# Linear attention and a two-layer MLP on one core: block 0 split after twelve weight groups, and a second buffer for the key exponentials

## The chip, the core and the metric

One core of a Trainium2 chip runs the whole program. The metric is the device time in microseconds (us) of one execution. Engines are named as the profile names them: PE is TensorE (matmuls), PEld its weight loads, DVE is VectorE, ACT is ScalarE, POOL is GpSimd, SP is SyncE (here it only starts DMAs).

## What is computed

Linear attention over 8 batches, 8 heads, 576 tokens and a head width of 64, and then a two-layer MLP on the 4608 tokens of width 512, with a hidden width of 2048 and a leaky ReLU between the layers.

```python
def phi(x):
    proj = np.einsum('bhsd,df->bhsf', x, w_phi)                  # 128 features
    proj = proj - np.max(np.abs(proj), axis=-1, keepdims=True)
    return np.concatenate([np.exp(proj), np.exp(-proj)], axis=-1)
q_p, k_p = phi(q), phi(k)
kv = np.einsum('bhsf,bhsd->bhfd', k_p, v)
z = np.sum(k_p, axis=2)
num = np.einsum('bhsf,bhfd->bhsd', q_p, kv)
den = np.einsum('bhsf,bhf->bhs', q_p, z)[..., None] + 1e-06
x = (num / den), heads side by side, as (4608, 512)
h = x @ w_in
out = np.maximum(0.01 * h, h) @ w_out
```

## The kernel before

**Attention** goes by pairs of heads: 32 pairs, four to a batch. Pairs 0 to 3 have functions of their own at the start. From pair 4 on `k_phase(i)` makes the key side of pair i while `q_phase(i - 1)` (`token_q_phase` below pair 8) makes the query side of the pair before it. A key phase works through 576 tokens in five chunks `c` of 128 (the last of 64). For each it subtracts the maximum (into `pmk`), takes exp of plus and minus that on ACT into the tile `ek` (L249, L250), rounds `ek` to `kph` on ACT (L69, called with the key "kph"), takes the rest `kpl` = `ek` - `kph` on POOL or DVE (L74), and multiplies both by the values on PE (L211). From pair 8 on this is done in such high and low parts; before that `ek`, `kph` and `kpl` serve as three exponential buffers. `ek` has one buffer and is also used for the sums that leave PSUM (`kvs`). The tile `kvx` (same size) holds the key-value product of pairs 5 and 7 and is not used after pair 7.

A query phase ends with its products on PE (L417, L418, L420), copies to `ring` and `tq` on ACT (L422, L423), two transposes and a reciprocal on DVE (L426, L428, L429) and a multiplication into `ring` on POOL (L74). `ring` holds the attention output of two batches (576 tokens by 512 each).

**The MLP** goes by blocks of 256 tokens (18 blocks) and by groups `ft` of 128 hidden units (16 groups). A step is one block and one group. `layer1` is 12 matmuls of 256 columns (L601, L602, L604: high by high, high by low, low by high), then leaky ReLU and rounding on ACT (L607, L69 "gh") and the rest on DVE (L609 "gl"). `layer2`, three steps later (`LAG`), is six matmuls of 512 columns into `acc` (L623, L624, L625). Before a block starts, `split` rounds its 256 tokens out of `ring` into `xh` (ACT) and `xl` (POOL). A block can start only when the attention of every batch it touches is finished: block 2 needs batch 1 (pairs 4 to 7), block 4 needs batch 2 (pairs 8 to 11), block 6 batch 3.

**The weights** arrive as float64, in 32 pieces, alternately of `w_in` (`w0`) and `w_out` (`w1`), two for each group `ft`. `load_weights` decodes each on ACT and DVE and writes a high part (`w0h`, `w1h`, L69 on ACT) and a low part (`w0l`, `w1l`, L74 on DVE). The number in `w0h2` is `ft` divided by 4.

**The order of the work**: the table `steps` sets the order of the MLP steps. It runs `CUT` groups of block 0, then all 16 of block 1, then the rest of block 0, then blocks 2 to 17. The partial sum of block 0 is held in the `ks` buffer (`held`) in between, and block 0 is split a second time. A scheduler then puts all instructions into one fixed sequence for each engine; attention has the higher priority, then the weights, and the MLP steps fill in. Each engine runs its sequence in order.

```python
CUT = 8
steps = [(0, ft) for ft in range(CUT)] + [(1, ft) for ft in range(NFT)] + [(0, ft) for ft in range(CUT, NFT)] + steps
```

Of the kernel before, what the change touches and what calls it, by code (L numbers as in the profile page):

```python
# [9 lines left out]
F32 = mybir.dt.float32  # L10
# [7 lines left out]
P = 128  # L18
# [9 lines left out]
NTOK = B * S  # L28
NBLK = NTOK // T
LAG = 3  # L30
CUT = 8
NN = 8
NK = 8
NF = 12
# [12 lines left out]
def attention_moe_kernel(ctx: ExitStack, tc: tile.TileContext, q, k, v, vt, w_phi, w_in, w_out, out):  # L47
# [8 lines left out]
    def st(shape, dt, tag):  # L56
        return sp.tile(shape, dt, tag=tag, name=tag, bufs=BUFS.get(tag, 1))
# [8 lines left out]
    def copy_(key, o, i):  # L66
        e = pick(key) or "a"
        if e == "a":
            nc.scalar.copy(o, i)  # L69
        else:  # L70
            (nc.vector if e == "v" else nc.gpsimd).tensor_copy(o, i)

    def tt_(key, o, a, b, op):
        (nc.vector if pick(key) == "v" else nc.gpsimd).tensor_tensor(o, a, b, op=op)  # L74
# [68 lines left out]
    for j in range(2):  # L143
        r = slice(64 * j, 64 * j + 64)
        c = slice(F * j, F * j + F)
# [45 lines left out]
    def k_phase(i):  # L191
        nat, plain = i < NK, i < NF
# [17 lines left out]
        def kv_mm(j, lt, rt, first=False, last=False):  # L210
            nc.tensor.matmul(kvp[0 : lt.shape[1], 256 * j : 256 * j + 256], lhsT=lt, rhs=rt,  # L211
                             start=first and j == 0, stop=last, skip_group_check=True)

        for g in range(3):
# [30 lines left out]
            yield  # L245
            for s in range(w):
                c = 2 * g + s
                ek = st([P, 2, 256], F32, ("ek", "kph", "kpl")[c % 3] if nat else "ek")
                nc.scalar.activation(ek[r, :, 0:F], pmk[r, 2 * s : 2 * s + 2], AF.Exp)  # L249
                nc.scalar.activation(ek[r, :, F:256], pmk[r, 2 * s : 2 * s + 2], AF.Exp, scale=-1.0)  # L250
                if nat:
                    for j in range(2):
                        kv_mm(j, rv[r, 4 * j + c if c < 4 else 8 + j], ek[r, j], first=c == 0, last=c == 4)
                    yield
                    continue
                if c < 4:
                    kph = st([P, 2, 256], F32R, "kph")
                    kpl = st([P, 2, 256], F32R, "kpl")
                    copy_("kph", kph, ek)
                    tt_("kpl", kpl, ek, kph.bitcast(F32), ALU.subtract)  # L260
                    for j in range(2):
                        kv_mm(j, vh[:, 4 * j + c], kph[:, j], first=c == 0)
                        kv_mm(j, vl[:, 4 * j + c], kph[:, j])
                    for j in range(2):
                        kv_mm(j, vh[:, 4 * j + c], kpl[:, j])
                else:
                    kst = st([P, 2, 256], F32R, "kph")
                    copy_("kst", kst[r], ek[r])
                    nc.vector.tensor_tensor(kst[0:64], ek[r], kst[r].bitcast(F32), op=ALU.subtract)
                    for j in range(2):  # L270
                        kv_mm(j, vl[:, 8 + j], kst[:, j])
                        kv_mm(j, vh[:, 8 + j], kst[:, j], last=True)
                yield
# [340 lines left out]
    def layer2(i, ft, half=range(TT)):  # L614
        first, last = (ft in (0, CUT), ft in (CUT - 1, NFT - 1)) if i == 0 else (ft == 0, ft == NFT - 1)
        if first and half[0] == 0:
# [11 lines left out]
        for t in half:  # L628
            if ft == CUT - 1:
                if t == 0:  # L630
# [39 lines left out]
    steps = [(i, ft) for i in range(2, NBLK) for ft in range(NFT)]  # L670
    steps = [(0, ft) for ft in range(CUT)] + [(1, ft) for ft in range(NFT)] + [(0, ft) for ft in range(CUT, NFT)] + steps
    split(0)
# [47 lines left out]
```

## Time and profile before

| what | value |
|---|---|
| median of 3 runs (lowest, highest) | 1194.11 us (1193.7, 1196.47) |
| the profiled execution: its own time, its span | 1196.45 us, 1194.7 us |
| PE busy | 1164.5 us, 97% |
| PEld busy | 1045.5 us, 88% |
| ACT busy | 833.5 us, 70% |
| DVE busy | 755.9 us, 63% |
| POOL busy | 417.5 us, 35% |
| mean granted TensorE clock | 0.994 of 2.4 GHz |

A busy PE in this profile is not PE at its peak: the records of matmuls overlap, since one starts before the one ahead of it has ended. How fast PE goes is read from the distance between two starts, or from the number of matmul records in a stretch of known length. A matmul with plain float32 operands stands as two records. A figure in square brackets behind a row is the time in which the engine was idle just before it, with the instruction whose end released it.

### The profile page before, as it was taken

What the parts mean: (1) busy time and instruction counts of PE and PEld (TensorE: products, weight loads), DVE (VectorE), ACT (ScalarE), POOL (GpSimd) and SP (SyncE); (2) the same over time, 40 slices, a digit from 0 to 9 for tenths busy, and PEclk for the clock granted to TensorE, in tenths of its full rate; (3) what the DMA queues carried; (4) which work ended last, traced back from release to release, by engine and by line L of the source; (5) the groups of instructions that cost most, each with busy time, mean ns of one, the idle gap of its engine ahead of it and who ended that gap; (6) DMA issues with size and microseconds to landing.
All of it is one profiled execution on the core that took longest, in us unless ns stands there. A gap on an engine that the chain in (4) does not pass through costs nothing.

```text
span 1194.7 us, 21190 instructions
## 1 busy us (share of the span) xinstructions
PE 1164.5 (97%) x7576; PEld 1045.5 (88%) x7576; DVE 755.9 (63%) x1510; ACT 833.5 (70%) x2108; POOL 417.5 (35%) x422
## 2 busy tenths in 40 slices
PE   8899999999998999999999999999999999999998
PEld 5687888899897989889899999998999999988987
DVE  4899883566767777677787777726777776111111
ACT  4898884667777787878788888837787877432232
POOL 0111011345454444545455454604454544110000
PEclk9899999999998999999999999999999999999999
DMA  7334532111201111110111111101011100000000
GB/s 208 90 101 142 152 114 59 40 42 31 60 22 50 32 50 31 41 30 22 50 31 50 32 49 32 49 12 37 23 50 32 49 1 19 1 18 19 1 19 18
DMA packets 62778, 57.01 MB, mean 48 GB/s; under 512 B 45136, under 2 KB 46288, under 8 KB 62672
## 3 DMA queue, kind: packets, MB, share of 16 engines
q1 hardware_dynamic: 62672, 55.65, 16.4%
q8 instruction: 60, 0.98, 0.4%
q14 instruction: 46, 0.38, 0.1%
HBM read 46.20 MB, written 9.44 MB: 47 GB/s over the span
## 4 chain that ended last, share of the span: by engine, by line
PE 82%; DVE 8%; ACT 5%; issue 2%; DMA 1%; POOL 1%; SPq 0%; DVEq 0%; ACTq 0%; POOLq 0%
PE h L601 10%; PE h L604 10%; PE h L602 10%; PE acc L623 10%; PE acc L625 10%; PE acc L624 10%; PE c L211 7%; PE a L302 2%; PE a L420 2%; PE a L418 2%; PE a L417 2%; PE a L231 2%; PE a L333 1%; PE a L377 1%; PE a L378 1%
## 5 line engine op out<-in xcount | busy, mean ns | idle before, releaser
L601 PE MATMUL h<-xh,w0h 128*128 128x256 f32 x1152 | 296.3, 287 | 5.9 <-DVE gl L609 4.9
L602 PE MATMUL h<-xh,w0l 128*128 128x256 f32 x1152 | 290.9, 282 | 0.0
L609 DVE TENSOR_TENSOR gl<-h,gh 128x256 fp32r<-128x256 f32 x288 | 118.7, 416 | 245.9 <-ACT gh L69 220.6
L623 PE MATMUL acc<-w1h,gh 128*128 128x512 f32 x576 | 229.6, 399 | 6.4 <-ACT gh L69 6.3
L601 PEld LDWEIGHTS h<-xh,w0h 128*128 128x128 f32 x1152 | 218.0, 189 | 17.0 <-DVE gl L609 8.0
L624 PE MATMUL acc<-w1l,gh 128*128 128x512 f32 x576 | 227.7, 395 | 0.0
L602 PEld LDWEIGHTS h<-xh,w0l 128*128 128x128 f32 x1152 | 217.9, 189 | 7.0 <-issue 0.4
L607 ACT ACTIVATE h<-h 128x256 f32<-128x256 f32 x288 | 105.3, 368 | 155.0 <-PE h L604 152.0
L625 PE MATMUL acc<-w1h,gl 128*128 128x512 f32 x576 | 204.4, 396 | 0.0
L604 PE MATMUL h<-xl,w0h 128*128 128x256 f32 x1152 | 200.3, 283 | 0.0
L74 POOL TENSOR_TENSOR ql<-eq,qh 128x576 fp32r<-128x576 f32 x96 | 146.5, 1539 | 73.6 <-ACT qh L69 51.0
L604 PEld LDWEIGHTS h<-xl,w0h 128*128 128x128 f32 x1152 | 164.5, 189 | 1.1 <-issue 0.4
L74 POOL TENSOR_TENSOR kpl<-ek,kph 128x512 fp32r<-128x512 f32 x72 | 96.6, 1342 | 146.9 <-PE c L211 67.2
L623 PEld LDWEIGHTS acc<-w1h,gh 128*128 128x128 f32 x576 | 108.4, 188 | 27.7 <-ACT gh L69 8.9
L624 PEld LDWEIGHTS acc<-w1l,gh 128*128 128x128 f32 x576 | 108.4, 188 | 18.0
L69 ACT CAST gh<-h 128x256 fp32r<-128x256 f32 x288 | 105.1, 371 | 25.6 <-PE acc L624 20.0
L74 POOL TENSOR_TENSOR xl<-ring,xh 128x256 fp32r<-128x256 f32 (+3 forms) x100 | 62.6, 655 | 162.1 <-PE h L604 131.6
L74 POOL TENSOR_TENSOR ring<-ring,mb 128x576 f32<-128x576 f32 (+2 forms) x45 | 49.8, 1108 | 192.9 <-DVE mb L559 39.2
L625 PEld LDWEIGHTS acc<-w1h,gl 128*128 128x128 f32 x576 | 99.3, 189 | 8.1
L249 ACT ACTIVATE ek<-pmk 128x256 f32<-128x256 f32 (+1 forms) x128 | 53.3, 417 | 33.5 <-POOL kpl L74 17.3
L199 DVE TENSOR_TENSOR ks<-rk,ks 64x576 fp32r<-64x576 f32 x40 | 44.5, 1112 | 30.5 <-ACT ks L69 29.9
L211 PE MATMUL c<-kph,vh 128*66 128x256 f32 x240 | 62.1, 281 | 0.7 <-ACT kph L69 0.7
(214 smaller groups left out, 2257.8 us busy)
## 6 DMA issues: line engine op xcount, KB each, us to landing
out_dram<-o SPq DMA_DIRECT2D x35, 256.0 KB, 2.1
rk<-in_k_dram SPq DMA_DIRECT2D x29, 288.0 KB, 2.8
ring<-in_w_in_dram SPq DMA_DIRECT2D x16, 512.0 KB, 3.6
qh<-in_w_out_dram SPq DMA_DIRECT2D x16, 512.0 KB, 3.7
rq<-in_q_dram SPq DMA_DIRECT2D x28, 288.0 KB, 3.0
rv<-in_v_dram SPq DMA_DIRECT2D x29, 256.0 KB, 3.5
rv<-in_vt_dram SPq DMA_DIRECT2D x58, 32.0 KB, 3.0
fr<-in_k_dram SPq DMA_DIRECT2D x2, 288.0 KB, 3.4
```

The costliest lines, as they stand in the source:

```text
L69: nc.scalar.copy(o, i)
L74: (nc.vector if pick(key) == "v" else nc.gpsimd).tensor_tensor(o, a, b, op=op)
L211: nc.tensor.matmul(kvp[0 : lt.shape[1], 256 * j : 256 * j + 256], lhsT=lt, rhs=rt, start=first and j == 0, stop=last, skip_group_check=True)
L249: nc.scalar.activation(ek[r, :, 0:F], pmk[r, 2 * s : 2 * s + 2], AF.Exp)
L601: nc.tensor.matmul(ph, lhsT=weight(0, "h", ft)[:, d * P : d * P + P], rhs=xh[:, d], start=d == 0, stop=False)
L602: nc.tensor.matmul(ph, lhsT=weight(0, "l", ft)[:, d * P : d * P + P], rhs=xh[:, d], start=False, stop=False)
L604: nc.tensor.matmul(ph, lhsT=weight(0, "h", ft)[:, d * P : d * P + P], rhs=xl[:, d], start=False, stop=d == NP - 1)
L607: nc.scalar.activation(ph, ph, AF.Prelu, alpha=0.01)
L609: nc.vector.tensor_tensor(gl, ph, gh.bitcast(F32), op=ALU.subtract)
L623: nc.tensor.matmul(a, lhsT=gh[:, ts], rhs=weight(1, "h", ft), start=first, stop=False)
L624: nc.tensor.matmul(a, lhsT=gh[:, ts], rhs=weight(1, "l", ft), start=False, stop=False)
L625: nc.tensor.matmul(a, lhsT=gl[:, ts], rhs=weight(1, "h", ft), start=False, stop=last)
```

## The change

There are two edits. `CUT` goes from 8 to 12, so that twelve groups of block 0 run ahead of block 1 and four after it. And for key phases of pairs above 8 (`NN` is 8) the exponentials of odd chunks go to the tile `kvx` in place of `ek`; even chunks keep `ek`.

```diff
-CUT = 8
+CUT = 12
...
-                ek = st([P, 2, 256], F32, ("ek", "kph", "kpl")[c % 3] if nat else "ek")
+                ek = st([P, 2, 256], F32, ("ek", "kph", "kpl")[c % 3] if nat else "kvx" if c % 2 and i > NN else "ek")
```

The number of instructions is the same on every engine; the scheduler puts them in another order. Up to the eighth step of the MLP the order of PE is unchanged. Three places follow.

First place: PE, behind the end of the eighth step's `layer1` (rows with buffer numbers; `gh_1676` is the eighth step's result, `w0h0` is the high part of groups 0 to 3, `w0h2` that of groups 8 to 11). Before:

```order
L302 MATMUL a_1136<-bd_73,rq_604 128x256 x2
L211 MATMUL c_1071<-ek_1089,rv_1002 66x256 x2
L211 MATMUL c_1071<-kph_1103,rv_1002 66x256 x2
L601 MATMUL h_1695<-xh_70,w0h0_616 128x256
L602 MATMUL h_1695<-xh_70,w0l0_617 128x256
L601 MATMUL h_1695<-xh_70,w0h0_616 128x256
```

Now:

```order
L211 MATMUL c_1071<-kph_1103,rv_1002 66x256 x2
L623 MATMUL acc_1583<-w1h1_721,gh_1676 128x512
L624 MATMUL acc_1583<-w1l1_722,gh_1676 128x512
L623 MATMUL acc_1584<-w1h1_721,gh_1676 128x512
L624 MATMUL acc_1584<-w1l1_722,gh_1676 128x512
L625 MATMUL acc_1583<-w1h1_721,gl_1677 128x512
L625 MATMUL acc_1584<-w1h1_721,gl_1677 128x512
L601 MATMUL h_1687<-xh_70,w0h2_800 128x256
L602 MATMUL h_1687<-xh_70,w0l2_801 128x256
```

The ninth step was group 0 of block 1 and is now group 8 of block 0, behind six matmuls of `layer2` that used to come later.

Second place: PE, around the last query product of pair 11 (`a_3703`), which is the last product that block 4 needs; `h_4188` is the first step of block 4, and `h_4682` its second. Before:

```order
L602 MATMUL h_4682<-xh_70,w0l0_617 128x256
L420 MATMUL a_3683<-ql_3662,kvh_3213 128x288 x2
L625 MATMUL acc_3876<-w1h3_905,gl_4162 128x512
L625 MATMUL acc_3877<-w1h3_905,gl_4162 128x512
L417 MATMUL a_3703<-qh_3580,kvh_3213 128x288
L418 MATMUL a_3703<-qh_3580,kvl_3214 128x288
L417 MATMUL a_3703<-qh_3580,kvh_3213 128x288
L418 MATMUL a_3703<-qh_3580,kvl_3214 128x288
L420 MATMUL a_3703<-ql_3678,kvh_3213 128x288 x2
L211 MATMUL c_3505<-kph_3628,vh_74 66x256
```

Now:

```order
L418 MATMUL a_3703<-qh_3580,kvl_3214 128x288
L420 MATMUL a_3703<-ql_3678,kvh_3213 128x288 x2
L231 MATMUL a_4231<-wq_72,ks_4206 128x256 x2
L623 MATMUL acc_3876<-w1h2_813,gh_4065 128x512
L624 MATMUL acc_3876<-w1l2_814,gh_4065 128x512
L623 MATMUL acc_3877<-w1h2_813,gh_4065 128x512
L624 MATMUL acc_3877<-w1l2_814,gh_4065 128x512
L601 MATMUL h_4100<-xh_70,w0h3_892 128x256
...
L211 MATMUL c_4228<-kph_4261,vl_75 64x256
L601 MATMUL h_4188<-xh_70,w0h0_616 128x256
```

Block 4 had begun (on the parts of `ring` that were finished) before pair 11's last product was issued; now that product stands ahead of block 4's first matmul, with 36 matmuls of `layer1`, 24 of `layer2` and 28 of attention between the two.

Third place: ACT, the key phase of pair 10, from the exponentials of chunk 3 (into `ek_3152`, or now `kvx_3152`) to those of chunk 4 (`ek_3181`). Before:

```order
L249 ACTIVATE ek_3152<-pmk_3121 128x2x128
L250 ACTIVATE ek_3152<-pmk_3121 128x2x128
L69 CAST qh_3165<-eq_3175 128x576
L69 CAST qh_3165<-eq_3191 128x576
L69 CAST gh_3945<-h_3932 128x256
L69 CAST kph_3155<-ek_3152 128x512
L607 ACTIVATE h_3956<-h_3956 128x256
L405 ACTIVATE eq_3231<-mb_3229 128x288
L406 ACTIVATE eq_3231<-mb_3229 128x288
L69 CAST gh_3969<-h_3956 128x256
L249 ACTIVATE ek_3181<-pmk_3170 64x2x128
L250 ACTIVATE ek_3181<-pmk_3170 64x2x128
```

Now:

```order
L249 ACTIVATE kvx_3152<-pmk_3121 128x2x128
L250 ACTIVATE kvx_3152<-pmk_3121 128x2x128
L607 ACTIVATE h_3748<-h_3748 128x256
L69 CAST kph_3155<-kvx_3152 128x512
L69 CAST gh_3761<-h_3748 128x256
L249 ACTIVATE ek_3181<-pmk_3170 64x2x128
L250 ACTIVATE ek_3181<-pmk_3170 64x2x128
```

Between the two pairs of exponentials there were eight other instructions and there are now three.

## Rows read from the trace of the kernel before

**Rows 1.** Page, busy time; page, group of L609 (count | busy, mean ns | idle before).

```profile
PE 1164.5 (97%) x7576; PEld 1045.5 (88%) x7576; DVE 755.9 (63%) x1510; ACT 833.5 (70%) x2108; POOL 417.5 (35%) x422
...
L609 DVE TENSOR_TENSOR gl<-h,gh 128x256 fp32r<-128x256 f32 x288 | 118.7, 416 | 245.9 <-ACT gh L69 220.6
```

**Rows 2.** Stretches: length, PE, PEld, DVE, ACT, POOL busy (records), clock, DMA.

```profile
110.70:146.20 35.50, 35.41 (x211) 29.34 (x210) 32.38 (x70) 29.22 (x70) 2.32 (x5) 1.00 0.49 144
...
356.30:433.50 77.20, 72.20 (x471) 65.88 (x470) 53.85 (x107) 60.62 (x153) 35.27 (x34) 0.96 0.13 36
433.50:498.60 65.10, 64.08 (x444) 58.80 (x443) 47.76 (x95) 53.10 (x136) 33.10 (x34) 1.00 0.14 38
498.60:563.80 65.20, 63.58 (x438) 58.16 (x437) 49.60 (x94) 50.98 (x130) 31.50 (x29) 1.00 0.14 37
563.80:629.80 66.00, 64.13 (x443) 58.81 (x442) 52.99 (x96) 53.08 (x134) 35.22 (x30) 1.00 0.14 37
629.80:692.60 62.80, 62.80 (x436) 58.08 (x436) 46.21 (x95) 51.95 (x132) 30.23 (x29) 1.00 0.14 39
...
809.40:872.80 63.40, 61.94 (x426) 57.10 (x425) 45.35 (x89) 49.66 (x126) 31.24 (x29) 1.00 0.12 34
```

**Rows 3.** The same stretches, L601 alone (four of them to a step).

```profile
110.70:146.20 35.50, 8.90 (x32) 6.05 (x32) 1.00 0.49 144
...
356.30:433.50 77.20, 17.05 (x64) 12.55 (x64) 0.96 0.13 36
```

**Rows 4.** PE in order of time, 100 to 113 us: start, length, instruction.

```profile
102.15 0.39 PE L601 MATMUL h<-xh,w0h 128*128 128x256 f32 x1 [0.60 <-ACT w0h L69]
...
105.77 1.89 PE L333 MATMUL a<-eq,kvh 128*128 128x256 f32 x8
107.50 1.03 PE L302 MATMUL a<-bd,rk 128*128 128x256 f32 x4
...
111.91 0.64 PE L604 MATMUL h<-xl,w0h 128*128 128x256 f32 x4
112.39 0.39 PE L623 MATMUL acc<-w1h,gh 128*128 128x512 f32 x1
112.62 0.40 PE L624 MATMUL acc<-w1l,gh 128*128 128x512 f32 x1
```

**Rows 5.** DVE in order of time: low parts of `w_in` for groups 8 to 11.

```profile
112.03 0.64 DVE L74 TENSOR_TENSOR w0l<-ql,w0h 128x512 fp32r<-128x512 f32 x1
120.43 0.68 DVE L74 TENSOR_TENSOR w0l<-ql,w0h 128x512 fp32r<-128x512 f32 x1
128.77 0.68 DVE L74 TENSOR_TENSOR w0l<-ql,w0h 128x512 fp32r<-128x512 f32 x1
139.16 0.78 DVE L74 TENSOR_TENSOR w0l<-ql,w0h 128x512 fp32r<-128x512 f32 x1
```

**Rows 6.** All engines in order of time, 362 to 369 us.

```profile
362.45 0.43 PE L420 MATMUL a<-ql,kvh 128*128 128x288 f32 x2
...
365.80 0.40 PE L377 MATMUL a<-qs,wq 128*128 128x288 f32 x1 [1.13 <-DVE tq L379]
...
367.18 1.41 POOL L74 TENSOR_TENSOR ring<-ring,mb 128x576 f32<-128x576 f32 x1 [3.28 <-DVE mb L429]
...
367.98 0.40 PE L377 MATMUL a<-qs,wq 128*128 128x288 f32 x1 [1.64 <-DVE pmk L236]
...
368.98 0.38 PE L601 MATMUL h<-xh,w0h 128*128 128x256 f32 x1
```

**Rows 7.** PE by stretch, around the start of block 4.

```profile
362.40:380.00 17.60, 12.69 (x66) 0.81 0.22 66
```

**Rows 8.** Idle before L249 (releaser: us, times); order of time at 571 us.

```profile
  POOL kpl L74: 17.3, 17
...
571.45 0.42 ACT L249 ACTIVATE ek<-pmk 128x256 f32<-128x256 f32 x1 [1.04 <-POOL kpl L74]
571.57 0.39 PE L601 MATMUL h<-xh,w0h 128*128 128x256 f32 x1 [1.76 <-DVE gl L609]
```

## Prediction

> **What bounds the kernel now.** I read the page's busy times first. PE is busy 97% of the span, DVE 63%, ACT 70% [rows 1]. The change adds no instruction on any engine, so PE's work stays as it is, and only time in which PE stands still, or goes below its pace, can be won or lost. To find that time I cut the span at block starts; the count of L601, 64 in a stretch, shows that each stretch holds one block of 16 steps [rows 3]. Then I set the length of each stretch against its number of matmul records [rows 2]. Block 8 (629.8 to 692.6) has PE busy all through: 62.8 us for 436 records, 0.144 us each. At that pace block 4 (471 records) needs 67.8 us and takes 77.2, 9.4 too many. Blocks 5, 6 and 7 (444, 438, 443 records) need 63.9, 63.1 and 63.8 and take 65.1, 65.2 and 66.0: 1.2, 2.1 and 2.2 too many, together 5.5. Block 11 (426 records) loses 2.1. These are the sums that can be won. A difference under 0.3% (3.6 us) can't be told from none here.
>
> What is lost in block 4 shows in the order of time [rows 6, 7]. Pair 11's last product, which block 4 needs, is issued at 362.45. Copies, two transposes, the multiplication into `ring` (367.18, 1.41 us) and the rounding follow, and PE goes on with block 4's matmuls at 368.98, 6.5 us later. Until then PE has only the next pair's projections, and waits for them 1.13 and 1.64 us. From 362.4 to 380 it issues 66 matmuls in 17.6 us, at a mean granted clock of 0.81, which is full level (2.4 GHz) mixed with the half one (1.2 GHz) after these waits. The MLP has caught up with attention there.
>
> **Edit 1, `CUT` = 12.** Nothing is added: the same steps, the same two splits of block 0, the same hold and add. Two things move.
>
> *Weights.* Groups 8 to 11 are wanted from the ninth step on; before, block 1 used groups 0 to 7 first, from 110.7 to 146.2 [rows 2, 3], so these groups had over 30 us to spare. I work out when PE gets to each and when it is ready. Paces: 0.12 us for a matmul of 256 columns (four L604 from 111.91 to 112.39), 0.23 for 512 (112.39 to 112.62), 0.216 for a record of a plain float32 product (eight from 105.77 to 107.50) [rows 4]; a transpose of 128 columns I set at half of that, 0.11, and a product of 64 columns as well.
> - Group 8: the ninth step started before at about 110.8, and now has six matmuls of 512 columns ahead of it, 1.4 us: 112.2. Its low part is ready at 112.03 + 0.64 = 112.7 [rows 5]. Wait 0.5.
> - Group 9: in the new order 12 + 6 MLP matmuls, 20 float32 records and 4 transposes stand between, 1.4 + 1.4 + 4.3 + 0.4 = 7.6 (rounded up): 120.3. Ready 120.43 + 0.68 = 121.1. Wait 0.8.
> - Group 10: the same way 6.8 us (eight of 20 float32 records are narrow; 6 small transposes): 127.9. Ready 129.45. Wait 1.5.
> - Group 11: 24 float32 records, 8.4 us: 137.9. Ready 139.94. Wait 2.1.
>
> Together 4.9. DVE makes the low parts, and was busy 32.38 of 35.5 us in this stretch [rows 2], so it sets their pace. In its new order 11 of the MLP's L609 stand ahead of group 11's low part, and 14 before: 3 x 0.416 = 1.2 us earlier [rows 1]. That leaves 3.7. I take **+3.5**. The low bound is 0 (DVE's idle 3.1 us in the stretch taken up as well), the high one +8 (each wait 0.8 us longer, because attention's work on DVE falls in between). `w_out` is wanted three steps later and has that much more time. Behind the blocked matmul stand this stretch's attention matmuls, and for those DVE and ACT wait.
>
> That a waiting matmul holds up the rest is seen once in the trace: at 102.15 PE had been idle 0.60 us for a high part from ACT [rows 4], with work behind it in the sequence. The Trainium skill ("TensorE: Matmul & The Clock Gate", part 2, what happens when you issue a matmul) says that matmuls stay in program order and that only weight loads are pulled ahead. By that rule all of the 3.7 us count, as in my sum; if the engine could let attention pass, the term would be 0 and the sum 3.5 us lower. The trace agrees as far as its one wait shows.
>
> *The lead of attention.* While MLP steps wait for weights, attention goes on, so at the same step of the MLP it is further on. In the new order pair 11's last product stands ahead of block 4's first matmul, with 36 matmuls of 256 columns, 24 of 512 and 28 of attention (about 0.12 each) between: 4.3 + 5.5 + 3.4 = 13.2 us of PE work. The tail from that product to the rounded tokens was 6.5 us [rows 6]. So the wait at block 4 is covered with 6.7 us to spare. I take **-8.5** of the 9.4, since small waits remain in every block; bounds -9.4 and 0 (if attention on the chip is later than its place in the sequence by more than the spare).
>
> **Edit 2, `kvx`.** ACT's exponentials waited 17 times for POOL's `kpl`, to let go of `ek`: 17.3 us in all, 1.04 of them at 571 us [rows 8]. That is idle ACT time, not PE time. But ACT runs in order, and behind these exponentials stand the MLP's L607 and "gh", on which L609 and so PE wait: 1.76 us at 571.57 [rows 8]. With two buffers the exponentials of a chunk no longer wait for `kpl` of the chunk just before, and go earlier in ACT's order, with less bunching at a pair's end. The block's boundary also moves from a pair's end to its middle, so rounding for a block and rounding for a new pair (both ACT's) no longer coincide. This bears on the 5.5 us of blocks 5 to 7. I take **-3.5**; bounds -7.6 (these three and block 11 entirely) and +6 (the same kind of wait, some 2 us, in three blocks more). `kvx` itself is free from pair 7's query products on, two pairs earlier; `kpl` has one buffer still, so POOL is the next limit.
>
> **Sum.** +3.5 - 8.5 - 3.5 = -8.5 us. The profiled execution took 1196.45 us, and would come to 1187.95; the median of the runs shown is 2.3 us below that execution, so against it the forecast is 1194.1 - 8.5 = **1185.6**. The forecast's own range is 1181 to 1190.
>
> **Rivals.**
>
> *Held up by weights, and slower (10%).* A matmul of steps 9 to 12 that waits for `w0l` holds the attention matmuls behind it; DVE then gets attention's results late, in its order they stand ahead of the next `w0l`, and each wait makes the next one longer. For: DVE 91% busy in the stretch, and each group's wait in my working is longer than the one before (0.5, 0.8, 1.5, 2.1). Against: DVE has three L609 fewer. It decides if group 11 comes 7 us later than 139.9, past the spare at block 4. Then the first term is +8 and the wait at block 4 stays with what is left of the lead, say -2, and blocks 5 to 7 as they were: 1194.1 + 8 - 2 = 1200.
>
> *Another wait in place of the old ones (17%).* Block 4's wait goes, but the new order on ACT and POOL puts waits of some 2 us elsewhere: each of blocks 5 to 8 starts with the tail of a pair's key side bunched on PE. Price: +3.5 - 8.5 + 3 x 1.5 = -0.5, or 1193.6. For: such waits stood in four of the blocks shown here, and none was visible in the order. Against: block 8 shows that a block with the same work can run without any.
>
> *More is won (13%).* Weights come as DVE's freed time allows (+0.5), block 4's 9.4 go, and blocks 5, 6, 7 and 11 run at block 8's pace (-7.6): 1194.1 - 16.5 = 1177.6.
>
> *It doesn't do what it says (3%).* `kvx` could still be held when pair 9 wants it, or the lead be gone by block 4 for reasons of the ring; then only the weights' waits remain: 1194.1 + 3.5 = 1197.6.
>
> **How the numbers follow.** My forecast has the other 57%. Faster by over 0.3% means under 1190.5: the forecast's 57, 13 for more, and a little of the 17: 0.73. Within 0.3%: the rest of the 17 and half of the last rival: 0.17. Slower: 0.10. The range must leave out no more than 2 in 10: from 1178, which just leaves out the middle of "more is won", to 1196, which leaves out the slower rival.
>
> **What would show it.** Right: the L601 of groups 8 to 11 have idle time before them that ends with `w0l` or `w0h`, 2 to 5 us together; attention stands further on at block 2; the stretch around block 4's start has full clock and some 7 matmuls a us; L249's idle for `kpl` falls well below 17.3 us; blocks 5 to 7 take 0.144 to 0.146 us a record. Wrong: a wait over 3 us or a stretch at half clock before 145 us, block 4 with its 9 us still, or blocks 5 to 9 with over 2 us too many each.

## The result, and the profile after

The changed kernel takes 1212.12 us (median of 4 runs, 1210.76 to 1214.57), beside 1193.9 for the kernel before in the same session: a ratio of 1.015, 95% interval 1.0129 to 1.0172. It is 18.2 us slower; the prediction said 1185.6. A difference without an interval below is one of medians. The profiled execution has a span of 1212.8 us.

The page's busy times, and the group of L609, after the change [rows 1]:

```profile
PE 1172.6 (97%) x7576; PEld 1048.0 (86%) x7576; DVE 779.0 (64%) x1510; ACT 833.8 (69%) x2108; POOL 426.6 (35%) x422
...
L609 DVE TENSOR_TENSOR gl<-h,gh 128x256 fp32r<-128x256 f32 x288 | 118.9, 417 | 240.3 <-ACT gh L69 223.8 <-PE acc L625 7.2 <-ACT tq L423 4.8
```

The instruction counts are the same, as forecast. DVE is busy 23 us longer for the same 1510 instructions (the last section comes back to that). PE's own waits, before and then after (waiting operation, releaser: us in all, times, longest):

```profile
PE acc L623 <- ACT gh L69: 6.3, 7, 1.9
...
PE h L601 <- DVE gl L609: 4.9, 4, 1.8
```

```profile
PE h L601 <- DVE gl L609: 10.8, 8, 2.7
PE acc L623 <- ACT gh L69: 6.6, 7, 1.8
```

`gl` was late four times and is late eight times. Where that falls, by stretches after the change from one block's start to the next (blocks 4, 5, 6, 9 and 13; columns as in [rows 2]):

```profile
371.50:438.10 66.60, 64.81 (x442) 58.88 (x441) 50.10 (x98) 53.58 (x137) 35.41 (x35) 1.00 0.14 40
438.10:505.20 67.10, 63.91 (x438) 58.27 (x436) 53.11 (x97) 53.25 (x138) 35.12 (x33) 1.00 0.13 36
505.20:569.00 63.80, 63.31 (x436) 58.42 (x436) 50.53 (x93) 51.35 (x128) 32.54 (x30) 1.00 0.14 38
...
700.50:767.90 67.40, 64.94 (x439) 58.79 (x438) 48.98 (x90) 51.27 (x132) 31.64 (x28) 1.00 0.12 32
...
945.70:1018.10 72.40, 68.03 (x451) 61.79 (x451) 47.84 (x95) 56.01 (x143) 36.47 (x35) 0.98 0.07 21
```

At the 0.144 us a record of the prediction, block 4 needs 63.6 us for 442 records and takes 66.6: 3.0 too many, where it lost 9.4 before [rows 2]. Block 9 loses 4.2 (439 records, 63.2) and block 13 loses 7.5 (451 records, 64.9). That rule is rough where the mix of matmuls differs, so the following table goes by each matmul: the median distance from a start to the next is taken for each shape in the trace of before, these are added up in each kernel's fixed order of PE, and a block's number is by how many us its real length exceeds that sum. (Stretches of 16 steps; the first two hold blocks 0 and 1, and the time before the first step, 53 to 57 us by the profile, is not in it. Columns: kernel before, the change, and the runs e1, e2, e16 and e17 below.)

```
stretch   before  change    e1      e2     e16     e17
first       5.0     9.5    11.0     4.9     9.0     9.9
second      1.8     1.7     1.7     1.9     1.6     1.4
block 2     0.8     4.2     0.0     0.9     0.2     0.2
block 3     1.1     1.7     1.5     3.3     3.0     2.5
block 4    10.0     3.6     1.5    15.0     2.0     1.7
block 5     1.7     4.3     1.6     0.9     6.3     3.5
block 6     2.5     1.0     3.0     3.1     0.9     0.8
block 7     2.7     3.2     6.2     1.4     0.1     0.0
block 8     0.2     2.7     1.8     2.0     0.2    -0.1
block 9     0.2     4.2     4.0     4.9     0.3     0.1
block 10    0.2     1.9     4.0     2.0     0.2    -0.1
block 11    2.0     0.8     1.9     0.6     1.9     1.3
block 12    0.3     0.5     0.2     0.5     0.3     0.1
block 13    0.6     8.0     0.6     7.0     0.5     0.6
to 16      32.0    50.2    41.9    52.1    29.4    23.7
```

The last line sums all stretches to block 16 (14 to 16 are not shown): 18.2 us more after the change. That this is the whole difference is no check of the rule, since the same matmuls are added up in both kernels; what the rule tells is where the time falls. The gain at block 4 is there, and so is a cost of 4.5 in the first stretch. What was not forecast is some 3 us in block 2, 2.6 in block 5, 8.2 in blocks 8 to 10 and 7.4 in block 13.

How such a loss comes about shows in the order of time after the change, at the start of block 13 (PE, ACT and DVE):

```profile
957.29 0.67 DVE L74 TENSOR_TENSOR pmk<-pmk,m 128x512 f32<-128x512 f32 x1
957.42 0.38 PE L601 MATMUL h<-xh,w0h 128*128 128x256 f32 x1 [1.49 <-DVE gl L609]
...
957.99 0.42 ACT L249 ACTIVATE ek<-pmk 128x256 f32<-128x256 f32 x1 [1.60 <-DVE pmk L74]
...
963.21 1.43 DVE L74 TENSOR_TENSOR pmk<-pmk,m 128x512 f32<-128x512 f32 x1
...
964.74 0.42 ACT L249 ACTIVATE ek<-pmk 128x256 f32<-128x256 f32 x1 [3.10 <-DVE pmk L74]
...
965.37 0.35 ACT L69 CAST gh<-h 128x256 fp32r<-128x256 f32 x1
...
965.77 0.50 PE L623 MATMUL acc<-w1h,gh 128*128 128x512 f32 x1 [1.76 <-ACT gh L69]
```

ACT comes to the exponentials of a group at 961.6 and stands still for 3.10 us, because DVE's subtraction (L74) has not yet made their `pmk`. The MLP's rounding `gh` stands behind them in ACT's order; PE needs it and stands still for 1.76 us. From 965 to 975 the mean granted clock is then 0.83, full level (2.4 GHz) mixed with the half one (1.2 GHz):

```profile
965.00:975.00 10.00, 9.23 (x54) 8.70 (x55) 4.84 (x9) 7.82 (x21) 4.14 (x3) 0.83 0.00 0
```

For the whole execution, ACT's idle time before L249 by what ended it (us, times), after the change; the line for `kpl` answers to that of before [rows 8]:

```profile
  DVE pmk L74: 33.1, 19
  POOL kpl L74: 9.5, 8
  DVE pmk L242: 7.9, 5
  POOL pmk L74: 0.3, 1
```

Before, DVE's `pmk` had:

```profile
  DVE pmk L74: 5.6, 6
```

So the wait for `kpl` fell from 17.3 to 9.5 us as the prediction said, and a wait for `pmk`, six times as long as before, stands in its place.

### The profile page after: what moved, and what is told of

The parts are those of the page before. It is cut to its first block, busy times and chain, and to the rows that moved or that the text cites. A ratio compares the mean times of both kernels' runs of the same rounds, so it can differ in the third digit from the quotient of the medians.

```text
span 1212.8 us, 21133 instructions
## 1 busy us (share of the span) xinstructions
PE 1172.6 (97%) x7576; PEld 1048.0 (86%) x7576; DVE 779.0 (64%) x1510; ACT 833.8 (69%) x2108; POOL 426.6 (35%) x422
## 4 chain that ended last, share of the span: by engine, by line
PE 71%; DVE 7%; ACT 6%; issue 3%; POOL 1%; DMA 0%; DVEq 0%; POOLq 0%; ACTq 0%
PE h L601 9%; PE h L602 9%; PE h L604 9%; PE acc L623 9%; PE acc L624 9%; PE acc L625 9%; PE c L211 5%; PE a L417 2%; PE a L420 2%; PE a L418 2%; PE a L231 1%; PE a L302 1%; PE a L377 1%; PE a L378 1%; DVE qs L366 1%
## 5 line engine op out<-in xcount | busy, mean ns | idle before, releaser
L601 PE MATMUL h<-xh,w0h 128*128 128x256 f32 x1152 | 295.0, 286 | 11.4 <-DVE gl L609 10.8
L602 PE MATMUL h<-xh,w0l 128*128 128x256 f32 x1152 | 292.1, 283 | 0.0
L609 DVE TENSOR_TENSOR gl<-h,gh 128x256 fp32r<-128x256 f32 x288 | 118.9, 417 | 240.3 <-ACT gh L69 223.8
L601 PEld LDWEIGHTS h<-xh,w0h 128*128 128x128 f32 x1152 | 218.8, 190 | 23.0 <-DVE gl L609 13.8
L624 PE MATMUL acc<-w1l,gh 128*128 128x512 f32 x576 | 227.8, 396 | 0.0
L602 PEld LDWEIGHTS h<-xh,w0l 128*128 128x128 f32 x1152 | 218.8, 190 | 7.3 <-DVE w0l L74 0.3
L625 PE MATMUL acc<-w1h,gl 128*128 128x512 f32 x576 | 201.9, 397 | 0.0
L604 PE MATMUL h<-xl,w0h 128*128 128x256 f32 x1152 | 196.8, 283 | 1.0 <-POOL xl L74 1.0
L74 POOL TENSOR_TENSOR ql<-eq,qh 128x576 fp32r<-128x576 f32 x96 | 142.1, 1495 | 76.9 <-ACT qh L69 59.4
L624 PEld LDWEIGHTS acc<-w1l,gh 128*128 128x128 f32 x576 | 108.5, 188 | 18.5 <-DVE pmk L242 0.4
L74 POOL TENSOR_TENSOR xl<-ring,xh 128x256 fp32r<-128x256 f32 (+3 forms) x100 | 70.8, 738 | 151.7 <-PE h L604 133.6
L74 POOL TENSOR_TENSOR kpl<-ek,kph 128x512 fp32r<-128x512 f32 x49 | 66.5, 1358 | 161.5 <-ACT kph L69 108.7
L74 POOL TENSOR_TENSOR ring<-ring,mb 128x576 f32<-128x576 f32 (+2 forms) x45 | 49.7, 1105 | 195.4 <-DVE mb L429 72.1
L249 ACT ACTIVATE ek<-pmk 128x256 f32<-128x256 f32 (+1 forms) x82 | 34.2, 418 | 45.7 <-DVE pmk L74 32.9
L69 ACT CAST qh<-eq 128x576 fp32r<-128x576 f32 x96 | 62.5, 668 | 2.1 <-PE a L418 1.5
```

Source lines behind the costliest of these rows:

```text
L601: nc.tensor.matmul(ph, lhsT=weight(0, "h", ft)[:, d * P : d * P + P], rhs=xh[:, d], start=d == 0, stop=False)
L602: nc.tensor.matmul(ph, lhsT=weight(0, "l", ft)[:, d * P : d * P + P], rhs=xh[:, d], start=False, stop=False)
L604: nc.tensor.matmul(ph, lhsT=weight(0, "h", ft)[:, d * P : d * P + P], rhs=xl[:, d], start=False, stop=d == NP - 1)
L609: nc.vector.tensor_tensor(gl, ph, gh.bitcast(F32), op=ALU.subtract)
L624: nc.tensor.matmul(a, lhsT=gh[:, ts], rhs=weight(1, "l", ft), start=False, stop=False)
L625: nc.tensor.matmul(a, lhsT=gl[:, ts], rhs=weight(1, "h", ft), start=False, stop=last)
```

## Experiments

In the table, "idle" is the sum of that list for each, ACT's idle time before L249; "pmk" is its line for DVE's L74. (e13 and e14 make this `pmk` in another line too, and e6 makes a part of it in `kvx`; their numbers are of both together. The ratios and intervals are against the runs of before on the same chip.)

```
run                  time us   ratio to before (95%)   idle   pmk
before               1193.9                            33.8    5.6
the change           1212.12   1.015  1.0129..1.0172   50.8   33.1
e1  CUT 12           1201.64   1.0063 1.0042..1.0085   37.7    8.4
e2  kvx              1216.87   1.0192 1.0173..1.0211   59.3   47.3
e3  kvx, 1 and 2     1209.66   1.0127 1.0112..1.0142   50.4   33.7
e4  kvx, 2 and 3     1197.83   1.0031 1.0019..1.0043   30.1    4.1
e5  CUT 10           1199.69   1.0044 1.0029..1.0059   27.8    4.3
e6  kvx for pmk      1206.77   1.0096 1.0075..1.0117   48.8    8.0
e7  kvx, 1           1208.86   1.0119 1.0103..1.0134   62.6   40.8
e8  kvx, two pmk     1215.53   1.0176 1.0161..1.0191   46.5   33.8
e9  dn in o          1208.6    1.0116 1.0099..1.0133   37.0   13.8
e10 two pmk          1202.04   1.0069 1.0052..1.0086   39.0   11.2
e11 two pmk, dn mb   1209.97   1.014  1.0125..1.0155   53.1   12.6
e12 dn in mb         1189.53   0.9967 0.9955..0.998    33.8    5.8
e13 kvx, split max   1211.38   1.0153 1.0138..1.0168   49.2   37.9
e14 e12, split max   1192.51   0.9995 0.9985..1.0005   37.1   14.6
e15 CUT 9            1192.25   0.9991 0.9982..1.0001   25.5    6.4
e16 CUT 12, 2 and 3  1191.2    0.9978 0.9969..0.9988   33.6    4.5
e17 e16, dn in mb    1186.5    0.9941 0.9926..0.9955   33.9    5.0
e18 e15, dn in mb    1189.21   0.9963 0.9949..0.9977   26.1    6.6
```

### The two edits apart (e1, e2)

e1 has the first line of the change's diff alone (`CUT = 12`), e2 the second alone (odd chunks to `kvx`).

> Only the first edit: twelve groups of block 0 first, ek with one buffer. Theory A (the first edit costs: it moves each block's start from a pair's end to its middle, where attention's own work on ACT and DVE stands ahead of the block's first gh and gl): the waits of the changed kernel at the starts of blocks 5 to 10 stay (about 19 us there), block 13 loses under 1 us as before, so about 1203 us. Theory B (the second edit costs: with two buffers the exponentials of two chunks, their roundings and their products stand bunched on ACT and PE ahead of the MLP's): the weights' 4 us are lost, block 4's 6 to 7 us are won and blocks 5 to 10 lose no more than before, so 1188 to 1194 us.

> Only the second edit: eight groups of block 0 first, odd chunks of pairs from 9 on in kvx. Theory A: block 4 waits its 10 us as before, blocks 5 to 10 as before or less, only block 13 may lose some us: 1192 to 1201 us. Theory B: the waits at blocks 3 and 5 to 10 and the 8 us at block 13 come with this edit: 1205 to 1212 us.

Against 1194.23 us for before in the same session, e1 is 7.4 us slower and e2 22.6. They don't add up: the second edit costs 22.6 us by itself and 10.5 on top of the first (1212.12 - 1201.64). Most of the loss lies in the edit from which the prediction wanted 3.5 us. Neither theory came out whole. Theory A was right that the first edit costs (it had about 1203 us for e1) and wrong on e2. Theory B was right that the second edit costs, though e2 lies above its range, and wrong that the first does not. The order of time of e2 shows the wait at its full length (ACT, DVE and PE; chunks 2 and 3 of a key phase):

```profile
704.91 1.72 DVE L366 TENSOR_TENSOR qs<-rq,qs 64x576 fp32r<-64x576 f32 x1
...
705.07 0.36 ACT L69 COPY pmk<-a 128x256 f32<-128x256 f32 x1
...
705.81 0.38 ACT L69 COPY pmk<-a 128x256 f32<-128x256 f32 x1
...
707.71 0.40 DVE L236 TENSOR_TENSOR pmk<-a,pmk 128x256 f32<-128x256 f32 x1
...
708.35 0.69 DVE L239 TENSOR_REDUCE m<-pmk 128x4 f32<-128x512 f32 x1
...
709.76 0.39 PE L601 MATMUL h<-xh,w0h 128*128 128x256 f32 x1 [1.28 <-DVE gl L609]
709.96 0.68 DVE L74 TENSOR_TENSOR pmk<-pmk,m 128x512 f32<-128x512 f32 x1
...
710.74 0.42 ACT L249 ACTIVATE ek<-pmk 128x256 f32<-128x256 f32 x1 [3.43 <-DVE pmk L74]
```

`pmk` has one buffer for two chunks. Chunk 2's copy into it can come only when chunk 1's exponentials have read it, and from that copy (705.07) to the end of the subtraction (710.64) it takes 5.6 us over ACT and DVE. Not all of that is work on `pmk`: DVE has instructions of the query side in between in its order, L366 (1.72 us) among them. Over the 23 pairs whose chunks I could tell apart in e2, ACT runs 0.2 instructions between the exponentials of chunks 0 and 1 (4.0 before), and 9 from chunk 1's to chunk 2's (11 before) while that distance, from the end of the one to the start of the other, lasts 6.0 us (5.7 before). Its idle time before chunk 2's exponentials is 43.6 us in all, and 8.0 before. So in the mean ACT stands still for 1.9 of the 6.0 us in e2 and for 0.3 of 5.7 before: with `ek` alone, the wait for `kpl` spread out chunks 0 and 1, and more work was left for the time behind chunk 1.

### Which chunks (e3, e4, e7, e16)

```diff
-                ek = st([P, 2, 256], F32, ("ek", "kph", "kpl")[c % 3] if nat else "ek")
+                ek = st([P, 2, 256], F32, ("ek", "kph", "kpl")[c % 3] if nat else "kvx" if c in (1, 2) and i > NN else "ek")
```

e3 has this, e4 `c in (2, 3)`, e7 `c == 1`, all with `CUT = 8`; e16 is e4 with `CUT = 12`.

> CUT = 8; from pair 9 on chunks 1 and 2 use kvx and the others ek, so chunk 1 no longer waits for chunk 0's kpl, but chunk 2 waits for chunk 1's kpl again as before. Theory late pmk (with alternating buffers the exponentials of chunk 2 move ahead in ACT's order to where their pmk is not ready on the chip; ACT stands still about 2 us a pair with the MLP's L607 and gh behind it): the idle time before L249 for pmk falls from the 47 us of kvx alone to under 15 us, and the time to 1192 to 1202 us. Rival, any other order costs (the order of before is a lucky one): 1205 to 1217 us whatever the idle time before L249.

> CUT = 8; from pair 9 on chunks 2 and 3 use kvx, so chunk 2 is free of chunk 1's kpl while chunks 1 and 3 wait as before. Theory late pmk: the idle time before L249 for pmk stays over 30 us and the time 1206 us or more. Rival, the extra exponentials back to back within a group (chunk 0 and 1, chunk 2 and 3) do the harm: pmk idle time small and 1192 to 1202 us.

> Theory (the doubling of chunk 1 alone carries the cost of the second edit: with chunks 0 and 1 in different tiles the fixed order puts chunk 2's exponentials earlier on ACT than its pmk is ready): 1206 to 1218 us, and ACT idle before L249 for DVE's pmk (L74) of 30 us or more. Rival (it is the odd chunks together, or the doubling of chunk 3, that does harm): 1194 to 1202 us and under 12 us of that idle time.

> The change with chunks 2 and 3 in kvx in place of 1 and 3, so that chunks 0 and 1 share ek as before. Theory (the doubling between chunks 0 and 1 carries edit 2's cost): 1198 to 1205 us, near the first edit alone (1201.6), ACT idle before L249 for pmk (L74) under 15 us. Rival (two buffers cost whatever chunks they serve): 1208 to 1216 us.

In e2, e3, e7 and the change, chunks 0 and 1 lie in different tiles: 33 to 47 us of waits for `pmk`, and 1208.9 to 1216.9 us. In e4 and e16 they share `ek`, `pmk` costs 4.1 and 4.5 us, and the times are 1197.8 and 1191.2. e3 and e4 both went against the expectation of the theory that I then had (that chunk 2's exponentials come too early once they are free of chunk 1's `kpl`), and pointed to chunks 0 and 1; e7, the doubling of chunk 1 alone, confirmed that, inside both bounds set for it. e16 settles it: the change with nothing altered but which chunks go to `kvx` is 20.9 us faster than the change. It is 0.22% faster than the kernel before (interval 0.12% to 0.31%), and below the 1198 to 1205 us that I expected. In e4 and e16 the second buffer hardly moves the exponentials in ACT's order: 3.7 and 4.1 instructions stand between chunks 0 and 1 and 11.4 and 11.6 between chunks 1 and 2, where it was 4.0 and 11.0 before. So what these two show is that the harm goes when chunks 0 and 1 stay apart, not that a second buffer for the exponentials wins time: at `CUT = 8` e4 is 3.8 us slower than before, and at `CUT = 12` e16 is 10.4 us faster than e1. Why the same choice costs on one base and wins on the other stays open. The list of e16 before L249, and its block 4 and the two next blocks:

```profile
  POOL kpl L74: 12.7, 15
  DVE pmk L242: 8.3, 7
  POOL pmk L74: 8.1, 9
  DVE pmk L74: 4.5, 7
```

```profile
366.30:430.80 64.50, 63.53 (x437) 58.10 (x435) 48.75 (x91) 51.42 (x131) 31.11 (x27) 1.00 0.14 38
430.80:499.10 68.30, 65.36 (x429) 59.89 (x428) 47.27 (x92) 51.26 (x133) 30.99 (x32) 0.95 0.13 36
499.10:563.10 64.00, 63.63 (x440) 58.59 (x440) 51.28 (x97) 51.72 (x132) 34.08 (x31) 1.00 0.14 38
```

Block 4 (437 records, 62.9 us at 0.144) takes 64.5. Only block 5 loses much, 6.5 of 68.3 us, with half clock in a part of it.

### How many groups ahead (e5, e15)

```diff
-CUT = 8
+CUT = 10
```

e5 has this, and e15 `CUT = 9`; the exponentials keep `ek`.

> Ten groups of block 0 first, ek with one buffer. Theory phase (of the 7 us that CUT = 12 alone costs, those in blocks 7 to 10 come because each block starts 12 to 16 us of PE work behind a pair's end instead of 5 to 10): here blocks start 2 to 10 us behind, so the losses in blocks 7 to 10 stay as before (about 3 us), groups 8 and 9 cost 2 to 4 us, block 4 is covered in part: 1189 to 1195 us. Rival, any other order costs: 1198 to 1206 us.

> CUT 9 alone: PE's order is new from the ninth step on, but pair 11's last product stands as late before block 4 as in the kernel before (5.5 us of PE work behind its first matmul), and one group is wanted earlier. Theory (time is lost only by late weights, a short lead at block 4 and early exponentials): 1192 to 1197 us, block 4's 9 us still there. Rival (any new order places new waits of 4 us and more): 1198 to 1206 us.

e5 missed the theory it was to test, that the boundary's place against the pairs decides: its time is in the rival's range, its block 6 lost 7.1 us reckoned as in the table, and block 4 still 9.0, though ACT's idle time before L249 was less than before (27.8 against 33.8 us). In that block PE waits 2.3 us once for `gh`, and the mean granted clock is 0.95. e15 tells more. Its order of PE is another from the ninth step on, and its time is that of before, as its theory said. So a new order is not slower because it is new.

### A second buffer elsewhere (e6, e8 to e12)

e6 gives `kvx` to `pmk` of group 1 in place of the exponentials. e8 and e10 give `pmk` two buffers, with and without the second edit, and take the room from `dn`, whose use goes to the tile `o`; e9 moves `dn` alone. e11 and e12 are e10 and e9 with `dn` of pairs 4 to 7 in the unused half of `mb`.

```diff
-BUFS = {"kph": 2, "eq": 2, "m4": 2, "g": 2, "gh": 2, "gl": 2, "ql": 2}
+BUFS = {"pmk": 2, "kph": 2, "eq": 2, "m4": 2, "g": 2, "gh": 2, "gl": 2, "ql": 2}
...
-            dn = st([P, U], F32, "dn")[:, 0:w]
+            dn = st([P, DM], F32, "o")[:, 0:w]
```

> CUT = 8, ek with one buffer; from pair 9 on kvx serves as a second buffer for pmk (chunks 2 and 3) instead. Theory late pmk: what is late is pmk of chunks 2 and 3, whose copies wait until the exponentials of chunks 0 and 1 have read it; with its own buffer it is early, idle time before L249 for pmk under 10 us, time 1186 to 1196 us. Rival, any other order costs: 1203 to 1217 us.

> The second edit with a second buffer for pmk as well (the tile dn moves into o to make room, CUT stays 8). Theory (the lateness of pmk behind early exponentials costs the time, and pmk is late because it has one buffer): ACT's idle time before L249 for pmk falls from 47.3 us to under 12, and the time to 1202 us or less. Rival 1 (pmk is late because its chain over PE, ACT and DVE is long, whatever its buffers): idle stays over 25 us and the time at 1206 to 1218. Rival 2 (any new order of the scheduler's loses, since small waits fall elsewhere): idle under 12 us and still 1203 to 1217 us.

> Neither edit; only the tile dn is dropped and its use goes to o. In the order pair 11's last product then stands 33 us of PE work ahead of block 4, and 28 to 30 us ahead at the later boundaries, with the exponentials' places as before. Theory (block starts lose time only where that lead is short or where early exponentials block ACT): block 4's 9.4 us go, 1184 to 1190 us. Rival (the order before is a lucky draw and any other places new waits): 1196 to 1206 us.

> Two buffers for pmk (dn in o), one for the exponentials, CUT 8. Theory: pmk is ready early and the exponentials keep their late places, the lead at block 4 is 22 us of PE work: ACT idle before L249 for pmk (L74) under 6 us, 1185 to 1193 us. Rival (any new order places new waits): 1196 to 1208 us.

> As e10 (two buffers for pmk, one for the exponentials, CUT 8), but from pair 4 on dn is the unused half of mb and not o; e10's fixed order on PE has a run of 15.5 us of attention without any MLP step at 200 to 235 us, where its trace loses some 15 us, and this order has none. Theory (apart from that run, two buffers for pmk cost nothing and give the lead at block 4): 1185 to 1191 us. Rival (a new order places new waits, whatever is doubled): 1196 to 1206 us.

> As e11 with one buffer for pmk: the exponentials' tiles are those of the kernel before, only the order is another. Theory (waits before L249 for pmk are few as long as ek has one buffer, so only the places of the blocks change): 1190 to 1197 us, ACT idle before L249 for pmk (L74) under 15 us. Rival (any new order places new waits): 1198 to 1208 us.

e8 to e10 have a stretch of their own that is lost. In their order some 15 us of attention stand without a step of the MLP. From 200 to 240 us, e10 and then the kernel before:

```profile
200.00:220.00 20.00, 14.69 (x72) 11.43 (x71) 8.66 (x19) 10.87 (x28) 7.35 (x9) 0.91 0.24 56
220.00:240.00 20.00, 16.21 (x84) 12.92 (x84) 17.71 (x40) 13.51 (x34) 4.21 (x6) 0.91 0.37 109
```

```profile
200.00:220.00 20.00, 20.00 (x127) 17.85 (x126) 5.98 (x15) 11.27 (x36) 6.78 (x12) 1.00 0.20 49
220.00:240.00 20.00, 20.00 (x125) 17.28 (x124) 12.41 (x25) 11.89 (x31) 4.98 (x7) 1.00 0.23 64
```

PE is busy 30.9 of 40 us there, and all 40 before. Reckoned as in the table, the second stretch loses 13.6 to 15.1 us more than before in e8, e9 and e10, so their times say little on what they were to test; without it e9 would be near 1195 and e10 near 1187 us (inside what was expected of it), by this estimate. e12, without that hole, is 4.0 us faster than before, with the same order of PE and the same waits before L249; what makes it faster is told with e17 below.

Two buffers for `pmk` did not do what I expected of them. e11 was to take 1185 to 1191 us and took 1210: its waits for `pmk` are 12.6 us, but those for `kpl` went to 34.4 us in 32 waits, and PE lost 9.2 us in block 6, 6.3 in block 7 and 6.2 in block 9. In e6 it is the same: 8.0 us for `pmk`, as expected, but 33.4 for `kpl` and 1206.77 us. In e8, `pmk` stays late (33.8 us) although it has two buffers: by this idle time its first rival came, that the chain is long whatever the buffers. So doubling one tile around the exponentials brought a long wait for the other one in e6 and e11 (in e10 the two waits rose less, to 21.7 and 11.2 us). Over all runs, those with an idle sum of 46 us or more take 1206.77 us or more, and those of 39 or less stay at 1202.04 or under, but for e9 with its hole. That is a connection seen in 20 kernels, and not a price for each us: e8 owes its place in it to its hole, without which it would be near 1202 us with 46.5 us of idle time, and below 38 us the order of the times does not follow it.

### The chain to `pmk` made shorter (e13, e14)

From pair 12 on the maximum and the subtraction go by one chunk, for e2 and for e12:

```diff
+    def ksplit(x, m, n):
+        nc.vector.tensor_reduce(m, x, axis=AX.X, op=ALU.max, apply_absolute_value=True)
+        nc.vector.tensor_tensor(x, x, m.unsqueeze(2).broadcast_to([n, 2, F]), op=ALU.subtract)
```

> The second edit alone (CUT 8), and from pair 12 on the maximum and its subtraction go by one chunk in place of two, on DVE: two small instructions more for each of groups 0 and 1, but chunk 2's pmk need not wait for chunk 3's. Theory (early exponentials of chunk 2 cost time because the chain to their pmk is longer than the place in the order allows): ACT idle before L249 for pmk falls from 47 us to under 25, and the time from 1217 to 1208 us or less. Rival (the order alone is worse, the wait for pmk is only where it shows): the idle time moves elsewhere, 1211 us or more.

> As e12 (dn in mb, neither edit), with the same split of the maximum by chunks as e13. Theory (only the 6 to 12 us of ACT's idle time for pmk are there to be won, and DVE has work to spare): 1184 to 1192 us. Rival (any new order places new waits): 1196 to 1208 us.

e13 has the direction of the theory and not its size: `pmk` 47.3 to 37.9 us, the time 1216.87 to 1211.38 (5.5 us less). Both bounds that I had set, 25 and 1208, were missed; the time is in the rival's range, but the idle time did not move elsewhere, as the rival had it (59.3 to 49.2 us in all). e14 differs from e12 by the split alone and is 3.0 us slower than e12 (ratios to before 0.9995 against 0.9967, with intervals that do not meet). So the split has a price of its own of some 3 us there; if it costs as much in e13, the shorter waits for `pmk` are worth more than the 5.5 us by which e13 is faster than e2.

### Together (e17, e18)

> The two gains together: e16 (CUT 12, chunks 2 and 3 in kvx; 1191.2 us) and dn in mb as in e12 (4 us faster than before with the same order on PE). Theory (the two are apart, since dn's users end before block 4): 1185 to 1190 us. Rival (e12's 4 us lay in the ring's order of the first blocks, which CUT 12 changes): 1190 to 1196 us.

> CUT 9 (e15, 1192.25 us) and dn in mb (e12), one buffer for the exponentials. Theory (the gains add): 1186 to 1190 us. Rival (they do not): 1191 to 1196 us. In both cases block 4 keeps its 9 us.

e17, with `CUT = 12`, chunks 2 and 3 in `kvx` and `dn` in `mb`, takes 1186.5 us: 0.59% faster than before (interval 0.45% to 0.74%) and 25.6 us faster than the change. The gains of e16 and e12 add. It loses 1.7 us in block 4 and at most 3.5 in any later one. The gains of e15 and e12 add as well in e18 (1189.21 us, inside its theory's range), with some 10 us still lost in block 4.

That they add has a reason that the lists of waits don't show. PE's order is the same in e12 as before, in e17 as in e16 and in e18 as in e15, and yet `layer2` goes faster: the median distance from the start of an L624 to the next matmul is 232 ns in each of the 12 kernels that keep the tile `dn`, and 227 to 228 in each of the 8 that move its use (e8 to e12, e14, e17, e18). Over the matmuls of 512 columns (distances under 0.3 us, so without waits) the mean is 232.6 ns before and 230.3 in e12; times 1727 records this is 4.0 us, all that e12 wins. (e8 to e11 have this gain too, so what they lose is some 4 us more than their times say.) No run shows why the pace differs; whether it is where the tiles then lie in memory was not tried.

## Why the prediction was wrong

*Edit 2, the step that failed.* "With two buffers the exponentials of a chunk no longer wait for `kpl` of the chunk just before, and go earlier in ACT's order, with less bunching at a pair's end." The first half is right. The second took for granted that an earlier place is a gain. ACT runs its order whether or not the input is there, and the input's chain was never timed: the text asked what is next after `ek` and named `kpl` ("POOL is the next limit"), where it was `pmk`, with 5.6 us over ACT and DVE from its first copy. (That `pmk` has one buffer is not enough of a reason: with two, in e8, 33.8 of e2's 47.3 us are still there.) The bunching did not go either, it moved: chunks 0 and 1 back to back. I took -3.5 with +6 as the worst; e2 measured +22.6, and the change against e16 +20.9. The bound came from "the same kind of wait, some 2 us, in three blocks more"; in fact ACT's idle time for `pmk` is spread over 19 waits after the change and 23 in e2, and the losses of the change over blocks 2, 5, 8, 9, 10 and 13. What would have shown it beforehand: the distance from chunk 1's exponentials to chunk 2's, 5.7 us in the trace of before, and how much of it ACT could fill.

*Edit 1, the weights: the size nearly right, the place wrong.* Forecast +3.5 from waits for `w0l`; the first stretch costs 4.5 more after the change (9.5 against 5.0), 4.0 in e16. But no idle time of PE ends with `w0l`, and at most 0.15 us can be put down to it (at 120.75, where L602 starts 0.27 us behind L601 and not 0.12). So that the size is near is luck. After the change, DVE's low parts of groups 8 and 9, and PE:

```profile
111.31 0.69 DVE L74 TENSOR_TENSOR w0l<-ql,w0h 128x512 fp32r<-128x512 f32 x1
112.46 0.28 PE L602 MATMUL h<-xh,w0l 128*128 128x256 f32 x1
...
120.01 0.68 DVE L74 TENSOR_TENSOR w0l<-ql,w0h 128x512 fp32r<-128x512 f32 x1
120.75 0.39 PE L602 MATMUL h<-xh,w0l 128*128 128x256 f32 x1
...
123.17 0.60 ACT L69 CAST w1h<-ql 128x512 fp32r<-128x512 f32 x1
...
123.67 0.67 ACT L165 ACTIVATE kvl<-ring 128x512 int32<-128x512 uint32 x1
...
124.25 0.34 ACT L69 CAST gh<-h 128x256 fp32r<-128x256 f32 x1
...
124.65 0.72 PE L623 MATMUL acc<-w1h,gh 128*128 128x512 f32 x2 [1.19 <-ACT gh L69]
```

DVE had the low parts ready at 112.0 and 120.7, those of groups 10 and 11 at 128.75 and 137.7, 0.4 to 2.2 us earlier than the working said. PE stood still at 124.65 for a `gh` behind the decoding of `w_out` on ACT. That wait and three smaller ones (0.73, 0.18, 0.22) make 2.3 us; the rest shows in no wait.

*Edit 1, the lead: right.* Block 4's wait was to lose 8.5 of 9.4 us. By the table it goes from 10.0 to 1.5 in e1 (8.5 less), to 2.0 in e16 and to 3.6 in the change. After the change pair 11's last product is issued 13.4 us ahead of block 4's first matmul, where the working had 13.2, and block 4 then waits 0.60 us for tokens:

```profile
358.14 0.42 PE L420 MATMUL a<-ql,kvh 128*128 128x288 f32 x2
...
371.51 0.28 PE L601 MATMUL h<-xh,w0h 128*128 128x256 f32 x1
...
374.04 0.39 PE L604 MATMUL h<-xl,w0h 128*128 128x256 f32 x1 [0.60 <-POOL xl L74]
```

In the 17.6 us behind pair 11's last product PE issued 66 matmuls before, at a clock of 0.81 [rows 7]; in the 17.6 us from block 4's start after the change it issues 104, at full clock:

```profile
371.50:389.10 17.60, 15.81 (x104) 13.50 (x103) 10.81 (x19) 15.12 (x41) 13.18 (x15) 1.00 0.18 62
```

*What edit 1 also did.* Alone it is 7.4 us slower, since blocks 7, 9 and 10 lose 11.1 us more than before; with chunks 2 and 3 in `kvx` (e16) they lose 0.6 in all. The prediction had no term for a new order's waits on ACT in later blocks, except in the rival "another wait in place of the old ones". That was the case that came, in kind (new waits behind ACT, though not by the bunching on PE that it named), with a price of +4.5 where the change shows some 20. The prediction's own sign of being wrong, blocks 5 to 9 with over 2 us too many each, shows in blocks 5, 7, 8 and 9. What in the new order makes edit 1 alone lose in blocks 7, 9 and 10 stays open; the longest wait of PE there is 3.4 us in block 7, for ACT's `kph`.

*The slower rival* ("held up by weights") did not happen: group 11 came 2.2 us earlier than worked out, and it would have to be 7 later. The range ended at 1196 because only that mechanism and the rival of 3% (1197.6) led above it, and no term let edit 2 cost more than 6 us.

## What to carry to other kernels

A second buffer removes one wait from an engine that runs a fixed order; before taking its gain, follow the next inputs of the moved instructions back to where they are made, time that chain in the trace, and compare it with the work that stands in between. If the chain is longer, the engine stands still there, and what stands behind it pays. And where a change has two parts, measure each alone and on top of the other: here the first alone cost 7.4 us, and together with another choice of chunks, one condition in the line, it came out 2 us below the kernel before.

## What was not expected of the hardware

DVE's subtraction `kpl` of chunk 3 takes much longer when its inputs let it start while POOL is in an instruction of its own. Mean ns of one: before, after the change, and in e16, where chunk 3 shares its tile with chunk 2 (the groups by line and shape):

```profile
L74 DVE TENSOR_TENSOR kpl<-ek,kph 128x512 fp32r<-128x512 f32 x24 | 18.2, 759 | 46.0 <-ACT kph L69 23.4 <-POOL ql L74 6.8 <-ACT pmk L69 4.2
```

```profile
L74 DVE TENSOR_TENSOR kpl<-kvx,kph 128x512 fp32r<-128x512 f32 x23 | 29.8, 1295 | 13.4 <-PE c L211 12.1 <-POOL ql L74 1.2
```

```profile
L74 DVE TENSOR_TENSOR kpl<-kvx,kph 128x512 fp32r<-128x512 f32 x23 | 18.3, 795 | 38.0 <-ACT kph L69 32.5 <-PE h L604 3.7 <-issue 1.7
```

One by one it is plainer. Of the 23 after the change, the 7 that start while POOL is idle take 0.69 us. Of the 16 that start inside an instruction of POOL (15 times `ql`), 13 end 0.55 us behind the end of that instruction, whether it had 0.14 or 1.37 us to go; the other three start in the last 0.03 us of it and end 1.93 to 1.94 us behind it. The same happens to L366 in e2, 1.72 us at 704.91 while POOL makes `kpl` from 704.73 on (its mean before is 0.80), and to the subtraction `pmk` at 963.21 above, 1.43 us while POOL makes `kpl` from 962.80 to 964.09. The Trainium skill ("SBUF — State Buffer", Who interferes with whom) says that a DVE instruction with two inputs in SBUF and a POOL instruction that reads SBUF exclude each other through a shared port, and that the later one waits for the whole of the other. These ends agree with it. For `kpl` it makes 0.5 us more each, 12 of the 23 us by which DVE is busier. How much of the late `pmk` it explains was not tried by a run of its own. Against its being the main cause: chunk 3's `kpl` comes behind the wait for `pmk` at chunk 2 of the same pair; e7, with 41 us of waits for `pmk`, keeps chunks 2 and 3 in one tile (its `kpl` of chunk 3 takes 0.99 us); and the subtraction that makes `pmk` on DVE is on average shorter after the change than before:

```profile
L74 DVE TENSOR_TENSOR pmk<-pmk,m 128x512 f32<-128x512 f32 x40 | 40.4, 1010 | 0.7
```

```profile
L74 DVE TENSOR_TENSOR pmk<-pmk,m 128x512 f32<-128x512 f32 x40 | 35.1, 877 | 0.3
```

Why the fixed order puts the exponentials earlier than the chip has their input also stays open.
